# Filling TensorE with wider matmuls between the x transposes and the first projection, with a new scheduler seed

## Chip, cores, metric

One core of a Trainium2 chip. The metric is the device time of one execution in microseconds (us): the median of several runs, all fast unless said otherwise. A profiled run also gives the span from its first to its last instruction, some 1.7 to 2 us shorter than the time.

## The reference

Memory-augmented attention in four segments of 512 tokens, a ReGLU feed-forward network on the same x, and a gate that mixes the two (S = 2048, D = 512, 32 heads, F = 1792, bf16):

```python
x = A_x
g = _sigmoid((x * gate_w).sum(-1, keepdims=True))
a = _A_ref(x, A_wq, A_wk, A_wv, A_wo, A_beta)     # 4 segments: softmax inside one, memory M, z between them
b = _B_ref(x, B_W_gate, B_W_up, B_W_down)         # relu(x @ W_gate) * (x @ W_up) @ W_down
return g * a + (1 - g) * b
# within _A_ref, after each segment s:
M = M + einsum('bhld,bhle->bhde', phi(ks), vs)    # the memory update needs phi(k) transposed
```

## The kernel before

The kernel doesn't fix its order by hand. It describes operations with what they read and write, and a list scheduler, run when the kernel is built, places them on the five engines from estimated durations. Among ready operations of equal priority it adds a random amount drawn from a seed. What comes out is one fixed order for each engine:

```python
sc = Sched(seed=912)
...
def jitter(self, op):
    j = self.jit.get(op.cidx)
    if j is None:
        j = self.jit[op.cidx] = self.rng.random() * 400.0
    return j
```

TensorE starts with fillers (matmuls of constants), transposes the first 512 rows of x against an identity, fills once more, broadcasts gate_w, and begins the q projection:

```python
def warm(m, n, k, b):
    def fn(e):
        for i in range(m):
            ins = e.matmul(PL[:, b, 0:n], lhsT=ones[128, 128], rhs=ones[128, n], start=True, stop=True)   # cut: const_aps
        return ins
    ...
xps, xcs = [warm(5, 512, 0, 3)], []
...                                            # 16 transposes in six groups, each waiting for its part of x
xps.append(warm(3, 128, 1, 2))
xps.append(pe(lambda e: e.matmul(PL[:, 2, :], lhsT=ones[0:1, :], rhs=V.oTt[0:1, :], start=True, stop=True), 300, ..., name="gwx"))
```

SyncE issues nearly all loads, in the order of its program and on one queue (q1 carried 17.69 of the 18.12 MB of the profile), and among them the transposes of phi(k), which are done by DMA, and the transposed x of later segments:

```python
load_gu(0); load_gu(1); load_x(1)
load("sp", ["wo"], V.wo[:], ...)
load("sp", ["wd"], V.wd[:], ...)               # W_down, 1.8 MB, needed only from the first output on
...
sps.append(dma("sp", lambda e, g=g: e.dma_start_transpose(V.phik[:, :, g*128:(g+1)*128], V.ek[:, g, :]), ...))
```

and the memory update (`mu`) is the first reader of the transposed phi(k) on TensorE. ScalarE issues three tiny loads ("touches") of W_gate, W_up and W_down, each waiting for the one before.

## Time and profile before

| | kernel before |
|---|---|
| time, median of 3 | 271.73 us (271.53 to 272.24) |
| span of the profiled run | 269.1 us |
| first q projection | 6.09 us |
| array at full speed from | about 9.5 us |
| the four transposes of phi(k) before the first memory update, issue to landing | 4.2 to 10.3 us |
| longest wait of TensorE after 1 us | 0.8 us, at 18.2 us |

The page, the projection's rows and the start of the chain are shown in the prediction. TensorE's waits (who waited, for whom, us in total, times, longest):

```profile
PE psA L876 <- issue: 2.4, 15, 0.2
PE psL L548 <- PEq L1018: 0.8, 1, 0.8
PE psL L744 <- ACT E L752: 0.8, 1, 0.8
```

The second line is the start of the program. The third is the wait of the scores (L744) for an exponential. The first is fifteen waits, 0.2 us at the longest.

### The profile page before, as it was taken

The page shows a single profiled execution, that of the slowest core. Times are in us where ns is not written, and L with a number is a line of the kernel's source. Part 1 is how long each engine was busy: PE and PEld are TensorE (multiplying, and loading weights), DVE is VectorE, ACT ScalarE, POOL GpSimd, SP SyncE. Part 2 cuts the span into 40 slices and gives each one's busy share as a digit, 9 for nine tenths or more (in the row PEclk, how much of TensorE's full clock was granted, in tenths as well). Part 3 has the DMA queues.
Part 4 walks back from the last instruction along what each step waited for, and adds up shares of the span by engine and source line. Part 5 has one row for each costly group of instructions (what it writes and reads, how often), then busy time and mean ns, then how long its engine had stood idle before and what let it go on. Part 6 is the DMA issues. An engine that isn't in the chain of part 4 may idle for free.

```text
span 269.1 us, 6773 instructions
## 1 busy us (share of the span) xinstructions
PE 260.4 (97%) x2821; PEld 117.3 (44%) x2859; DVE 186.9 (69%) x372; ACT 186.5 (69%) x163; POOL 112.0 (42%) x227
## 2 busy tenths in 40 slices
PE   8989999999999999999999999999999999999996
PEld 3434454444444444444444444444444444444444
DVE  5678796988877497889986858776964437577400
ACT  4368898787799787676877696776776657774122
POOL 3014654486337533864276333822282235421000
PEclk9999999999999999999999999999999999999999
DMA  5899994410023223111012130100212000000011
GB/s 179 230 389 200 322 132 73 97 32 19 23 44 63 49 70 88 50 25 21 2 44 58 41 78 28 39 0 2 44 39 60 20 22 22 0 2 2 0 40 39
DMA packets 34208, 18.12 MB, mean 67 GB/s; under 512 B 23937, under 2 KB 33922, under 8 KB 34178
## 3 DMA queue, kind: packets, MB, share of 16 engines
q1 hardware_dynamic: 34048, 17.69, 27.9%
q8 instruction: 22, 0.36, 0.6%
q14 instruction: 8, 0.07, 0.1%
q10 hardware_dynamic: 130, 0.01, 0.0%
HBM read 9.75 MB, written 2.11 MB: 44 GB/s over the span
## 4 chain that ended last, share of the span: by engine, by line
PE 87%; DMA 4%; SPq 3%; issue 2%; DVE 1%; ACT 1%; ACTq 0%
PE psA L876 36%; PE psA L915 18%; PE psL L744 8%; PE psA L646 7%; PE psA L803 6%; PE psA L908 5%; PE psA L644 3%; DMA adT<-in_B_W_up_dram 2%; SPq L501 1%; PE psA L709 1%; PE psA L811 1%; DMA wq<-in_A_wq_dram 1%; DMA gexpT<-gscr 1%; SPq L670 1%; PE psA L691 1%
## 5 line engine op out<-in xcount | busy, mean ns | idle before, releaser
L752 ACT ACTIVATE E<-psL 128x2048 bf16<-128x2048 f32 x72 | 135.0, 1876 | 30.7 <-PE psL L744 30.3
L770 POOL TENSOR_SCALAR_AFFINE_SELECT E<-E 128x256 bf16<-128x256 bf16 x128 | 52.6, 436 | 105.4 <-ACT E L752 94.3
L876 PE MATMUL psA<-xT,wg 128*128 128x512 bf16 x216 | 57.7, 380 | 1.2 <-issue 1.1
L876 PE MATMUL psA<-xT,wu 128*128 128x512 bf16 x213 | 57.3, 379 | 1.4 <-issue 1.3
L915 PE MATMUL psA<-wd,hT 128*128 128x512 bf16 (+2 forms) x228 | 52.0, 366 | 0.9 <-issue 0.6
L788 POOL TENSOR_SCALAR_AFFINE_SELECT E<-E 64x512 bf16<-64x512 bf16 (+1 forms) x64 | 42.1, 686 | 18.8 <-ACT E L752 10.6
L887 DVE TENSOR_TENSOR hT<-psA,rl 128x512 bf16<-128x512 f32 x56 | 38.2, 682 | 12.1 <-PE psA L876 10.2
L915 PEld LDWEIGHTS psA<-wd,hT 128*128 128x128 bf16 x238 | 21.5, 98 | 23.3 <-issue 1.7
L822 DVE STREAM_TRANSPOSE Tn<-psA 128x512 f32<-128x512 f32 x32 | 21.0, 695 | 14.5 <-PE psA L811 14.3
L876 PEld LDWEIGHTS psA<-xT,wu 128*128 128x128 bf16 x224 | 20.4, 98 | 24.1 <-issue 1.7
L876 PEld LDWEIGHTS psA<-xT,wg 128*128 128x128 bf16 x224 | 19.9, 98 | 24.7 <-issue 2.7
L744 PE MATMUL psL<-qT,kp 32*128 32x64 bf16 (+3 forms) x768 | 28.7, 245 | 0.8 <-ACT E L752 0.8
L884 ACT ACTIVATE rl<-psA 128x512 bf16<-128x512 f32 x28 | 16.7, 596 | 15.6 <-PE psA L876 14.9
L744 PEld LDWEIGHTS psL<-qT,kp 32*128 32x128 bf16 x768 | 9.9, 92 | 31.0 <-issue 18.7
L925 ACT ACTIVATE osb<-psA,omg 128x512 bf16<-128x512 f32 (+2 forms) x13 | 8.5, 655 | 19.9 <-PE psA L908 13.2
L885 DVE TENSOR_SCALAR rl<-psA 128x512 bf16<-128x512 f32 x28 | 19.2, 686 | 4.0 <-PE psA L876 3.2
L646 PE MATMUL psA<-xT,wq 128*128 128x512 bf16 x63 | 17.8, 412 | 0.1
L663 DVE TENSOR_SCALAR kp<-kT,pm 128x512 bf16<-128x512 bf16 (+1 forms) x33 | 11.2, 357 | 9.0 <-PE psL L744 6.8
L803 PE MATMUL psA<-E,vaug 128*17 128x192 bf16 (+3 forms) x512 | 17.0, 273 | 0.1
L646 PE MATMUL psA<-xT,wk 128*128 128x512 bf16 x62 | 16.0, 380 | 0.2 <-issue 0.2
L908 PE MATMUL psA<-wo,oT 128*128 128x512 bf16 (+2 forms) x65 | 15.8, 366 | 0.4 <-issue 0.3
L644 PE MATMUL psA<-wv,xT 128*128 128x512 bf16 x61 | 14.7, 380 | 0.4 <-issue 0.3
(77 smaller groups left out, 235.3 us busy)
## 6 DMA issues: line engine op xcount, KB each, us to landing
out_dram<-osb SPq DMA_DIRECT2D x15, 128.0 KB, 1.8
wg<-in_B_W_gate_dram SPq DMA_DIRECT2D x8, 224.0 KB, 5.7
wu<-in_B_W_up_dram SPq DMA_DIRECT2D x8, 224.0 KB, 5.9
wd<-in_B_W_down_dram SPq DMA_DIRECT2D x1, 1792.0 KB, 10.5
osb<-in_A_x_dram SPq DMA_DIRECT2D x12, 128.0 KB, 2.2
vsh<-vaug SPq DMA_DIRECT2D x4, 272.0 KB, 3.0
hT<-in_A_x_dram SPq DMA_DIRECT2D x4, 128.0 KB, 2.2
wq<-in_A_wq_dram SPq DMA_DIRECT2D x4, 128.0 KB, 3.2
```

The costliest lines, as they stand in the source:

```text
L644: ins = e.matmul(A(ep)[:, :], lhsT=V.xT[:, kt, tok + col * 128:tok + (col + 1) * 128], rhs=w[:, kt, :], start=(kt == 0), stop=(kt == KT - 1))
L646: ins = e.matmul(A(ep)[:, :], lhsT=w[:, kt, col * 128:(col + 1) * 128], rhs=V.xT[:, kt, tok:tok + 512], start=(kt == 0), stop=(kt == KT - 1))
L744: ins = q.matmul(PL[:, jj, o:o + w], lhsT=kap(jj), rhs=V.qT[32 * jj:32 * jj + 32, qs, q0:q0 + w], start=True, stop=True, tile_position=(32 ...
L752: acts.append(act(lambda a, eout=eout: a.activation(eout, PL[:, :, :] if slot is None else PL[:, :, :].rearrange("q h (g c) -> q h g c", g ...
L770: pools.append(pool(lambda g, ap=ap: g.affine_select(out=ap, in_=ap, compare_op=ALU.is_ge, fill=0.0, base=64, pattern=[[0, 4], [1, 64]], c ...
L788: pools.append(pool(lambda e, ap=ap, base=base: e.affine_select(out=ap, in_=ap, compare_op=ALU.is_ge, fill=0.0, base=base, pattern=[[0, 8] ...
L803: ins = q.matmul(A(eps[p])[32 * jj:32 * jj + 17, 512 - w:512], lhsT=V.vaug[:, s % 2, j, 8 * G + 2 * jj + p, :], rhs=V.E[:, e, jj, o:o + w] ...
L822: ds.append(dve(lambda e, p=p, ep=eps[p]: e.transpose(V.Tn[:, p, :], A(ep)[:, :]), t_dve(512), writes=[f"Tn{p}"], name=f"tr{s}_{G}_{p}", e ...
L876: ins = e.matmul(A(ep)[:, :], lhsT=w[:, kt, f * 128:(f + 1) * 128], rhs=V.xT[:, kt, c * 512:(c + 1) * 512], start=(kt == 0), stop=(kt == K ...
L887: evs.append(dve(lambda e, ep=eu, r=r, hs=hs: e.tensor_tensor(V.hT[:, hs, :], A(ep)[:, :], V.rl[:, r, :], ALU.mult), t_dve(512), reads=[f" ...
L908: ins = e.matmul(A(ep)[:, 0:c1 - c0], lhsT=V.oT[:, o0 + G, i * 128:(i + 1) * 128], rhs=V.wo[:, G, c0:c1], start=st_ and G == 0, stop=sp_ a ...
L915: ins = e.matmul(A(ep)[:, 0:c1 - c0], lhsT=V.hT[:, slots[f], i * 128:(i + 1) * 128], rhs=V.wd[:, f, c0:c1], start=st_ and f == f0, stop=sp ...
```

## The change

The intent: up to about 9.5 us TensorE takes 0.427 us for 512 columns, later 0.215 (half speed and full speed), and the change bets that steadier work brings the switch forward. So fill TensorE without a break from the last transpose to the first projection. The 3 x 128 columns ahead of the broadcast go; 512 + 128 + 128 columns come behind it, into a bank of psA that is spare at that time, and with them comes a new seed.

```diff
-    sc = Sched(seed=912)
+    sc = Sched(seed=949)
...
-    xps.append(warm(3, 128, 1, 2))
     xps.append(pe(lambda e: e.matmul(PL[:, 2, :], ...), 300, reads=["oTt"], writes=["bankL2"], name="gwx"))
+
+    def warm1(e):
+        for n in (512, 128, 128):
+            ins = e.matmul(PA[:, 3, 0:n], lhsT=nc.const_aps.tensor(1.0, [128, 128], BF16), rhs=nc.const_aps.tensor(1.0, [128, n], BF16), start=True, stop=True)
+        return ins
+    xps.append(pe(warm1, 400, reads=["init3"], writes=[], name="warm1"))
```

## The prediction

In it "warm" is full speed as measured, 0.215 us for 512 columns. The 0.107 us for 128 columns is the pace at half speed: two transposes of x start at 3.142 and 3.249 us of the same trace. Point 4 and the sum weigh three cases for the switch: ahead of the first projection, 1.1 us earlier than it was (from 4.97 us, where the broadcast would start, to 6.09), and unmoved.

> **What bounds the kernel now.** I read the page first: busy shares, then the slices.
>
> ```profile
> PE 260.4 (97%) x2821; PEld 117.3 (44%) x2859; DVE 186.9 (69%) x372; ACT 186.5 (69%) x163; POOL 112.0 (42%) x227
> PE   8989999999999999999999999999999999999996
> PEclk9999999999999999999999999999999999999999
> ```
>
> TensorE works in nearly every slice; it is idle for 269.1 - 260.4 = 8.7 us of the span. The table of 10 us stretches puts 0.9 of that before 10 us, 0.8 between 10 and 20, 2.4 after 260 (the last outputs draining), so 4.6 us over the 240 us between. The program order is fixed, TensorE is the bound, and a gain must either make matmuls shorter or close idle time. The granted clock says full speed everywhere; whether the matmuls run at full speed has to be read from their own durations. So next the line of the first projections, in the stretches 6 to 9.3 us and 9.6 to 14 us (min/median/max ns):
>
> ```profile
> L646 PE MATMUL psA<-xT,wq x8: 606/631/631, 6.1 to 9.1; 128*128 128x512 bf16 x8
> L646 PE MATMUL psA<-xT,wk x11: 379/379/379, 11.3 to 13.6; 128*128 128x512 bf16 x11
> ```
>
> The same shape takes 631 ns first and 379 ns later. These durations overlap; the pace is read from the weight loads, one per matmul, in the timeline (start, us, what, idle before):
>
> ```profile
> 8.20 0.15 PEld L646 LDWEIGHTS psA<-xT,wq 128*128 128x128 bf16 x1 [0.28 <-issue]
> 8.63 0.15 PEld L646 LDWEIGHTS psA<-xT,wq 128*128 128x128 bf16 x1 [0.28 <-issue]
> 9.05 0.15 PEld L646 LDWEIGHTS psA<-xT,wq 128*128 128x128 bf16 x1 [0.28 <-issue]
> 9.48 1.45 PEld L646 LDWEIGHTS psA<-xT,wq 128*128 128x128 bf16 x7 [0.28 <-issue]
> ```
>
> One per 0.427 us up to 9.48, then seven in 1.45 us, about 0.215 each. The array switches from half to full speed near 9.5 us. Counted back: eight matmuls from 6.12 to 9.53 are slow, the remaining eight of the q projection and everything later is fast. What TensorE did before that, in its timeline:
>
> ```profile
> 0.84 2.29 PE L548 MATMUL psL<-const-bfloat16-1.0 128*128 128x512 bf16 x5 [0.84 <-PEq L1018]
> 2.96 2.21 PE L556 MATMUL psL<-ident,hT 128*128 128x128 bf16 x16
> 4.97 0.52 PE L548 MATMUL psL<-const-bfloat16-1.0 128*128 128x128 bf16 x3
> 5.42 0.60 PE L567 MATMUL psL<-oTt,const-bfloat16-1.0 1*128 1x512 bf16 x1
> 6.09 1.46 PE L646 MATMUL psA<-xT,wq 128*128 128x512 bf16 x3
> ```
>
> Filler, 16 x transposes, filler, the broadcast of gate_w, the first projection. TensorE "busy" hides gaps here[...]. At 0.427 us for 512 columns the broadcast that starts at 5.42 has streamed by 5.85, so the array stands empty 0.24 us until 6.09. Last, the chain of waits up to 18 us:
>
> ```profile
> 2.66 3.38 DMA wq<-in_A_wq_dram
> 6.09 4.05 PE psA L646 x10
> 10.17 5.21 DMA adT<-in_B_W_up_dram
> 15.41 0.36 ACTq L479
> 15.81 0.60 ACT kT L651
> 16.41 1.78 ACT E L752
> 18.23 0.40 PE psL L744 x8
> ```
>
> The first projection starts when the first piece of wq lands (6.04), not when the filler ends. Ten of its matmuls lead to the first q copy on ScalarE; just beside it ScalarE issues a 1 KB load (10.17), whose landing 5.21 us later holds up ScalarE's queue, then a k copy, the first exponential and the second group of scores at 18.23. So the half-speed stretch is on the path that sets the early part, with a nearly fixed delay behind it.
>
> [...] the new filler waits for the memset of bank 3 of psA; the four memsets begin at 0.99 and take 2.11 us, so they are over by 3.1 and the wait costs nothing at 5.4. No later accumulation is hurt, as each starts anew.
>
> **The change part by part.**
> 1. Removed: three fillers of 128 columns between the last transpose and the broadcast. 3 x 0.107 = 0.32 us of streaming; with the change of weights the broadcast started 0.45 us after them.
> 2. Moved: the broadcast comes up to about 4.97, 0.45 us earlier. Its copy on ScalarE (6.06) and the gate products on VectorE (6.69) can come 0.4 to 0.5 us earlier. Neither is on the chain above, so this is worth 0.
> 3. Added: 512 + 128 + 128 columns after the broadcast, 0.427 + 2 x 0.107 = 0.64 us at half speed. Together 0.427 + 0.64 = 1.07 us from 4.97: it ends at 6.04 to 6.1, against the first wq at 6.04. So the first projection moves by 0 to 0.1 us, and if the array is warm already it does not move at all.
> 4. What it is for: [...] eight matmuls at 0.215 instead of 0.427, 8 x 0.212 = 1.7 us gained. [...] the switch comes 1.1 us earlier, and half of that, 0.55 us, is gained. If neither, 0.
> 5. Does the gain get through? wq pieces are issued 0.47 us apart and land 3.0 to 3.4 us after issue, about 6.0 to 7.5; a warm q needs one per 3 x 0.215 = 0.65 us, so it keeps up. wk, issued from 4.56, lands by about 9.3, and a warm q ends at 6.12 + 16 x 0.215 = 9.55, so k keeps up too. The q copy, the 1 KB load behind it and ScalarE's release then move up with it, unless the load is queued behind others and lands at the same time. I take two thirds to all.
> 6. The seed of the scheduler: 912 becomes 949. It changes the random tie-breaks among ready instructions of equal priority on all engines, over all 250 us after. The work on TensorE is the same; what moves is the 4.6 us of scattered idle time plus the early 0.8 us and the tail. I put it at a mean of about +0.2 us gained (a seed is presumably picked because it did well) and a spread of 1 us either way, an estimate from the size of that idle time.
>
> Sum: for the switch, chances of 0.35 for 1.7 us, 0.4 for 0.55 and 0.25 for 0, i.e. 0.8 us; let through for the most part, 0.7; less 0.05 for a late start; plus 0.2 for the seed: about 0.9 us. Of 271.73 that leaves 270.8; I round down to 270.7, since the load behind the q copy may land in less than its 5.21 us when asked for earlier.
>
> **The rivals.**
> - The start is bound by the transfers: wq at 6.04 sets the first projection whatever the filler does, and the 1 KB load's landing sets ScalarE. For it: the chain shows both. Against: between them stand ten matmuls, 4.05 us, eight of them at half speed. If the load lands at 15.4 anyway, the change gives 0 to 0.3 us: 271.4 to 271.8.
> - The filler is too long and holds up the first projection, with the switch at the old time. For it: only 0 to 0.1 us of slack. It would cost at most 0.1 us: 271.8.
> - The seed outweighs the clock: another order makes TensorE wait for an exponential or a bank a few times more or less. For it: these waits are already small and many, the longest on TensorE 0.8 us. It could give 270 to 273 without any effect of the filler.
> - [...] the runs before, 271.53 to 272.24, and the profiled one, 270.94, spread over 1.3 us[...]. Then a median of three carries some 0.4 us of luck.
>
> **Range and chances.** A full early switch with a good seed is 271.7 - 1.7 - 1.2 = 268.8; no effect and a poor seed is 272.2. The range is 268.9 to 272.2. Two per cent is 5.4 us; the slow stretch in all is worth 1.7 us and all of the early idle time not 2, so neither side is likely: faster 0.02, same 0.96, slower 0.02.
>
> **What would show it.** In the changed profile: the broadcast near 4.97 and fillers until about 6.05, no gap before 6.09; weight loads of the first projection at 0.43 us for fewer than eight matmuls[...]; the first q copy at 8.5 to 9.6 instead of 10.17; the 1 KB load's landing and the second group of scores earlier by as much. If the copy comes early but the scores at 18.2 do not move, the transfer hides the gain. If everything up to 20 us is alike and the time differs, it is the seed, and TensorE's idle time after 20 us (8.7 - 1.7 = 7.0 us now) shows by how much. I am wrong if the time leaves the range, above all upward through a new wait in the middle.

## The result, and the profile after

| | before | changed |
|---|---|---|
| time, median of 6 runs each | 271.92 us (271.53 to 272.7) | 269.74 us (269.05 to 270.7) |
| ratio | | 0.9917, 95% interval 0.9892 to 0.9942 |
| span of the profiled run | 269.1 us | 267.3 us |

Ratios here and below are the mean time of one kernel's fast runs over the mean of the other's in the same rounds, so they are not quite the ratio of the medians. The change gains 2.2 us, 0.8%: inside the predicted range, and over twice the predicted 1.0 us.

At first sight the profile shows just what was intended. The page's first line and slices of the changed kernel:

```profile
PE 262.7 (98%) x2859; PEld 117.2 (44%) x2859; DVE 189.1 (71%) x371; ACT 187.6 (70%) x164; POOL 112.3 (42%) x227
PE   8999998999999999999999999999999999999996
PEclk9999999999999999999999999999999999999999
```

and its weight loads on TensorE (start, us, what, idle before):

```profile
5.02 0.09 PEld L566 LDWEIGHTS psL<-oTt,const-bfloat16-1.0 1*128 1x128 bf16 x1
5.33 0.33 PEld L570 LDWEIGHTS psA<-const-bfloat16-1.0 128*128 128x128 bf16 x3 [0.23 <-issue]
5.63 3.18 PEld L651 LDWEIGHTS psA<-xT,wq 128*128 128x128 bf16 x16
```

All sixteen q matmuls stand about 0.215 us apart, none 0.427: the array is fast from the first projection on. But look at the first two lines. The broadcast of 512 columns starts at 5.02, and 0.31 us later the fillers (L570) start: at half speed 512 columns alone take 0.427 us. (The record of the broadcast itself is 0.38 us long, against 0.60 in the kernel before.) The array was already fast when the first of the new fillers began. In this run the switch was not their work.

The chain up to 18 us has no wait for a transfer any more, only TensorE itself:

```profile
5.41 0.44 PE psA L570 x3
5.84 6.04 PE psA L651 x28
11.89 0.33 PE psL L749 x8
```

The last thing to see is what the early start buys. The first k projection's weights are loaded at 8.92 instead of 11.05 us, 2.1 us earlier, and the wait for the exponential at 18.2 us is gone. Together that is 2.9 us, yet the span shrinks by 1.8. The list of TensorE's waits says where the rest went:

```profile
PE psL L548 <- PEq L1023: 0.8, 1, 0.8
PE psA L651 <- DMA xT<-in_A_x_dram: 0.8, 1, 0.8
PE psA L808 <- DVE vaug L678: 0.5, 1, 0.5
```

At 43.5 us it waits 0.8 us for the transposed x of the third segment, and at 47.0 us 0.5 us for a copy on VectorE: new waits, 1.3 us. Part of the gain is given back.

This list is complete, and the fifteen waits for "issue" have no counterpart in it. The reason stands in the page's first line: 2859 matmul records for 2859 weight loads here, 2821 for 2859 in the kernel before. Those 0.2 us "waits" are holes left by the 38 missing records, not idle time.

### The profile page after: what moved, and what is told of

Its sections match the earlier page's. It is cut to its first block, busy times and chain, and to the rows that moved or that the text cites.

```text
span 267.3 us, 6812 instructions
## 1 busy us (share of the span) xinstructions
PE 262.7 (98%) x2859; PEld 117.2 (44%) x2859; DVE 189.1 (71%) x371; ACT 187.6 (70%) x164; POOL 112.3 (42%) x227
## 4 chain that ended last, share of the span: by engine, by line
PE 94%; SPq 2%; DVE 2%; DMA 1%; issue 0%; ACT 0%
PE psA L881 37%; PE psA L920 19%; PE psA L651 9%; PE psL L749 8%; PE psA L808 6%; PE psA L913 5%; PE psA L649 4%; PE psA L816 1%; DMA xT<-in_A_x_dram 1%; PE psA L714 1%; SPq L501 1%; SPq L675 1%; PE psL L548 1%; PE psA L696 1%; PE psL L556 0%
## 5 line engine op out<-in xcount | busy, mean ns | idle before, releaser
L881 PE MATMUL psA<-xT,wg 128*128 128x512 bf16 x224 | 59.6, 380 | 0.0
L881 PE MATMUL psA<-xT,wu 128*128 128x512 bf16 x224 | 59.3, 380 | 0.0
L920 PE MATMUL psA<-wd,hT 128*128 128x512 bf16 (+2 forms) x238 | 54.0, 367 | 0.0
L892 DVE TENSOR_TENSOR hT<-psA,rl 128x512 bf16<-128x512 f32 x56 | 38.1, 680 | 13.3 <-PE psA L881 12.6
L889 ACT ACTIVATE rl<-psA 128x512 bf16<-128x512 f32 x32 | 19.1, 597 | 17.0 <-PE psA L881 16.9
L930 ACT ACTIVATE osb<-psA,omg 128x512 bf16<-128x512 f32 (+2 forms) x12 | 7.8, 652 | 18.0 <-PE psA L913 13.2
L890 DVE TENSOR_SCALAR rl<-psA 128x512 bf16<-128x512 f32 x24 | 16.5, 688 | 3.5 <-PE psA L881 2.4
L651 PE MATMUL psA<-xT,wq 128*128 128x512 bf16 x64 | 16.2, 380 | 0.8 <-DMA xT<-in_A_x_dram 0.8
L913 PE MATMUL psA<-wo,oT 128*128 128x512 bf16 (+2 forms) x68 | 16.5, 367 | 0.0
L649 PE MATMUL psA<-wv,xT 128*128 128x512 bf16 x64 | 15.5, 380 | 0.0
L668 DVE TENSOR_SCALAR kp<-kT,pm 128x512 bf16<-128x512 bf16 (+1 forms) x33 | 12.3, 387 | 4.1 <-PE psL L749 3.8
```

The lines of the kernel that those rows point to most:

```text
L649: ins = e.matmul(A(ep)[:, :], lhsT=V.xT[:, kt, tok + col * 128:tok + (col + 1) * 128], rhs=w[:, kt, :], start=(kt == 0), stop=(kt == KT - 1))
L651: ins = e.matmul(A(ep)[:, :], lhsT=w[:, kt, col * 128:(col + 1) * 128], rhs=V.xT[:, kt, tok:tok + 512], start=(kt == 0), stop=(kt == KT - 1))
L881: ins = e.matmul(A(ep)[:, :], lhsT=w[:, kt, f * 128:(f + 1) * 128], rhs=V.xT[:, kt, c * 512:(c + 1) * 512], start=(kt == 0), stop=(kt == K ...
L892: evs.append(dve(lambda e, ep=eu, r=r, hs=hs: e.tensor_tensor(V.hT[:, hs, :], A(ep)[:, :], V.rl[:, r, :], ALU.mult), t_dve(512), reads=[f" ...
L913: ins = e.matmul(A(ep)[:, 0:c1 - c0], lhsT=V.oT[:, o0 + G, i * 128:(i + 1) * 128], rhs=V.wo[:, G, c0:c1], start=st_ and G == 0, stop=sp_ a ...
L920: ins = e.matmul(A(ep)[:, 0:c1 - c0], lhsT=V.hT[:, slots[f], i * 128:(i + 1) * 128], rhs=V.wd[:, f, c0:c1], start=st_ and f == f0, stop=sp ...
```

## The experiments

Twelve kernels ran in three calls of four. Those of one call share a chip and the runs of the kernel before. "Switch" is the time at which the spacing of the weight loads of q goes from 0.43 to 0.215 us, read from the one profiled run of each kernel; where all sixteen are at 0.215 ("early"), it came before the first.

| run | order of | fillers | median us | ratio to before | span | switch |
|---|---|---|---|---|---|---|
| before | before | old | 271.73 | 1 | 269.1 | 9.5 |
| changed kernel | change | new | 269.74 | 0.9917 | 267.3 | by 5.3 |
| newsched_oldfill | change | old | 269.54 | 0.9932 | 267.8 | 9.9 |
| oldsched_newfill | before | new | 271.09 | 0.9988 | 269.2 | 10.0 |
| newsched_nofill | change | none | 269.06 | 0.9918 | 268.1 | 9.8 |
| after_again | change | new | 269.53 | 0.9929 | 268.8 | 9.8 |
| newsched_dense | change | denser | 269.38 | 0.9901 | 267.6 | early |
| newsched_nofill_xT_touch | change | none | 270.01 | 0.9926 | slow | early |
| newsched_dense_xT_touch | change | denser | 271.46 | 0.9963 | 270.6 | early |
| oldsched_touch | before | old | 272.2 | 0.9998 | 271.3 | early |
| oldsched_wd | before | old | 268.04 | 0.9868 | 266.0 | early |
| newsched_nofill_wd | change | none | 267.5 | 0.9860 | 266.4 | early |
| before_again | before | old | 272.48 | 1.0018 | 270.7 | early |
| before_seed949 | a third one | old | 276.41 | 1.0169 | 274.8 | early |

The runs of the kernel before had medians of 271.55, 272.27 and 271.14 us in the three calls.

### First call: order against fillers

The change does two things, and the seed reorders every engine. To part them, the order must be held fixed while the fillers change. That is possible because the scheduler sees only the estimated duration of an operation, not what it emits. So the fillers were put inside operations that exist anyway; the resulting instruction lists are the same on all engines but for the fillers. (`ones` stands for the constant operands in the diffs, which are shortened.) This gives all four cells of order and fillers.

**newsched_oldfill**, the changed kernel's order with the old fillers:

```diff
-    xps.append(pe(lambda e: e.matmul(PL[:, 2, :], ...), 300, ..., name="gwx"))
+    xps.append(pe(lambda e: [*[e.matmul(PL[:, 2, 0:n], ones, ones) for n in (128, 128, 128)], e.matmul(PL[:, 2, :], ...)][-1], 300, ..., name="gwx"))
-        for n in (512, 128, 128):
+        for n in (8,):
```

> The changed kernel's instruction order on every engine (seed 949), but the fillers as in the kernel before: three of 128 columns ahead of the gate_w broadcast, and only one of 8 columns behind it. If the fillers work (they warm the array's clock earlier in most runs), this gives back most of the 2.2 us: 271.0 to 272.0, and in the profile half-speed projections (0.43 us apart) until 8.5 to 10 us. If the new order does the work, it stays at the changed kernel's 269.7, within 0.4 us. [...]

Measured: 269.54 us (269.01 to 270.25), ratio 0.9932 with an interval of 0.99 to 0.9964. The change's gain without the change's fillers.

**oldsched_newfill**, the old order with the new fillers:

```diff
-            for i in range(m):
-                ins = e.matmul(PL[:, b, 0:n], ...)
+            for i in range(m if k == 0 else 1):
+                ins = e.matmul(PL[:, b, 0:n if k == 0 else 8], ...)
-    xps.append(pe(lambda e: e.matmul(PL[:, 2, :], ...), 300, ..., name="gwx"))
+    xps.append(pe(lambda e: [e.matmul(PL[:, 2, :], ...), *[e.matmul(PA[:, 3, 0:n], ones, ones) for n in (512, 128, 128)]][-1], 300, ..., name="gwx"))
```

> The order of the kernel before on every engine (seed 912), but the fillers of the change: 8 columns ahead of the broadcast, 512 + 128 + 128 behind it. If the fillers work: 270.0 to 270.8, and fewer than eight slow projections in the profile. If the order does the work: 271.9 as before, within 0.4 us.

Measured: 271.09 us (270.47 to 272.48), ratio 0.9988, interval 0.9949 to 1.0027: the time of before.

**newsched_nofill**, nothing but 8 columns after the broadcast:

```diff
-        for n in (512, 128, 128):
+        for n in (8,):
```

> The changed kernel without any filler between the last transpose and the first projection but one of 8 columns; all orders as in the changed kernel. If filling that stretch matters for the clock, this is the slowest of the new order: 1 us or more above the changed kernel (270.7 to 271.7)[...]. If it does not, 269.4 to 270.0.

Measured: 269.06 us (268.85 to 269.96), ratio 0.9918. Without any filler it is no slower than with them.

**after_again**, the changed kernel unaltered:

> The changed kernel unaltered, for a second profile and for times on the same chip in the same rounds. Median 269.7 within 0.4. [...] the switch to full speed will not stand at 5.0 us again as in the first profile, but anywhere between 4.5 and 8.5.

Measured: 269.53 us (268.03 to 270.68), ratio 0.9929. The expectation of the switch failed: it came at 9.8 us, later than the 4.5 to 8.5 it named. The same kernel that was fast from its first projection had its first eight q matmuls at half speed here. Its weight loads:

```profile
9.16 0.15 PEld L651 LDWEIGHTS psA<-xT,wq 128*128 128x128 bf16 x1 [0.28 <-issue]
9.58 0.15 PEld L651 LDWEIGHTS psA<-xT,wq 128*128 128x128 bf16 x1 [0.28 <-issue]
9.90 1.39 PEld L651 LDWEIGHTS psA<-xT,wq 128*128 128x128 bf16 x7 [0.17 <-issue]
```

Those of newsched_oldfill, for comparison:

```profile
9.47 0.15 PEld L651 LDWEIGHTS psA<-xT,wq 128*128 128x128 bf16 x1 [0.28 <-issue]
9.89 1.18 PEld L651 LDWEIGHTS psA<-xT,wq 128*128 128x128 bf16 x6 [0.27 <-issue]
```

All four kernels of this call, with four kinds of filling, switch between 9.8 and 10.0 us. So two things follow. The order carries the gain, at either filling. And in these profiles the fillers don't set the switch: it stands nearly still, whatever fills the stretch.

What the order does in these late-switch runs shows only in part. The spans of the old order are 269.1 and 269.2, of the new one 267.8, 268.1 and 268.8: 0.9 us in the mean. TensorE waits for an exponential near 18 to 20 us in the old order 0.8 and 0.9 us, in the new one not at all, 0.4 and 0.7 us. In the old order two more spots, at 123 and 173 us, have two weight loads 0.51 us apart instead of 0.22, 0.3 us each; they are absent in the new order. But 0.9 is not 2.2; the clocks of the runs without a profile, at the end of the experiments, close part of the gap.

### Second call: force an early switch, and look behind it

Theory at this point: the early switch happens in some runs, and its gain is partly swallowed at 43 us. **newsched_dense** fills the gaps between the transposes, so that TensorE stops less there (from 3.04 to 5.24 us its weight loads show no stop, those of newsched_nofill three, of 0.27, 0.22 and 0.20 us); the change's own fillers shrink to 8 columns, as in newsched_nofill:

```diff
+FILLS = {"xt2": (192, "L"), "xt3": (160, "L"), "gwx": (128, "A"), "warm1": (128, "A")}
     for g in gs:                      # groups of waits and one operation, in program order
+        if e == "pe" and _name(g) in FILLS:
+            _fill(eng, sc, *FILLS[_name(g)])     # a matmul of ones, ahead of the operation's waits
         yield from g
```

> The changed kernel's orders, with fillers in the gaps between the x transposes (192 and 160 columns ahead of the third and fourth, 128 on either side of the broadcast) in place of the change's 512 + 128 + 128. [...] this should bring the switch to full speed forward from 9.6 to 9.9 us (five of six profiles so far) to 5 to 6.6 in the profile. If that early switch goes through to the end, 1 us or more below the kernel without fillers (269.06): 267.6 to 268.4. If it is swallowed by the transposed loads of x that the third segment waits for at 43 us, 268.6 to 269.4 with a wait there. [...]

Measured: 269.38 us (269.22 to 269.9), ratio 0.9901, the switch early. Its waits on TensorE:

```profile
PE psA L651 <- DMA xT<-in_A_x_dram: 0.6, 1, 0.6
PE psA L808 <- DVE vaug L678: 0.5, 1, 0.5
PE psA L696 <- DMA phik<-ek: 0.2, 1, 0.2
```

The expectation "swallowed" holds: 0.9901 is not clearly below the 0.9918 of the kernel without fillers (its interval reaches from 0.9886 to 0.995), and x is waited for. But the early switch can't be credited to the fillers, since the other three kernels of this call, one of them with the old fillers untouched, were early too. Whether denser filling moves a late switch is not tested: no dense kernel ran where the others were late.

Two more kernels of this call add edits off TensorE. ScalarE's wait for the landing of the W_up touch comes seven instructions later ("touch"), and the third segment's transposed loads are issued ahead of the second pair of phi(k) transposes ("xT"):

```diff
+    if e == "act":
+        n = [i for i, g in enumerate(gs) if _name(g) == "ldadT"][-1]
+        held, gs[n] = gs[n][:-1], gs[n][-1:]
+        gs[n + 7] = held + gs[n + 7]
+    if e == "sp":
+        x = [g for g in gs if _name(g).startswith("ldx2_")]
+        gs = [g for g in gs if g not in x[1:]]
+        n = gs.index(x[0])
+        gs[n + 1:n + 1] = x[1:]
```

**newsched_nofill_xT_touch**:

> No fillers, the changed kernel's orders, but for two edits off TensorE: ScalarE waits for the landing of the W_up touch seven instructions later, and the queue of SyncE issues the last three transposed loads of the third segment's x ahead of two transposes of phi(k). If ScalarE's wait for the touch is what stops TensorE near 18 to 20 us (0.3 to 0.9 us), 268.5 or so, against 269.06 without the edits, and no stall above 0.3 us there. If that wait is beside the path: 269.0 within 0.4.

Measured: 270.01 us over all runs, ratio of the fast ones 0.9926. A miss in us, and by its ratio the two edits together changed nothing against newsched_nofill's 0.9918.

**newsched_dense_xT_touch**:

> Both: the denser fillers and the two edits. If the early switch of the clock is real and was swallowed at 43 us, this is the fastest of all, 267.0 to 267.8, with no wait for x at 43 us. If the switch does not come early, as the kernel without fillers and with the edits, or 0.2 us slower.

Measured: 271.46 us, ratio 0.9963: meant to be the fastest and 2 us slower than newsched_dense. The expectation was wrong, and the trace shows something useful. Its weight loads:

```profile
39.65 0.11 PEld L649 LDWEIGHTS psA<-wv,xT 128*128 128x128 bf16 x2 [0.21 <-DVE mutmp L699]
42.76 0.48 PEld L696 LDWEIGHTS psA<-vaug,phik 128*128 128x128 bf16 x8 [3.00 <-issue]
43.20 0.37 PEld L649 LDWEIGHTS psA<-wv,xT 128*128 128x128 bf16 x3
43.75 0.15 PEld L649 LDWEIGHTS psA<-wv,xT 128*128 128x128 bf16 x1 [0.17 <-issue]
44.18 0.15 PEld L649 LDWEIGHTS psA<-wv,xT 128*128 128x128 bf16 x1 [0.28 <-issue]
```

Putting x first made the second pair of phi(k) late (the chain has one issued at 38.95 us and landed at 41.40; the changed kernel issues the pair from 33.81 us); TensorE stood still before the memory update (L696), 2.5 us by the list of its waits, and afterwards the loads are 0.43 us apart: the array has fallen back to half speed. Here a long wait cost twice, once as idle time and once as slow matmuls.

**oldsched_touch**, the old order with the ScalarE edit alone:

> The kernel before with one edit: ScalarE waits for the landing of the W_up touch seven instructions later; the order of every engine is the same. If the stall of TensorE at 18.2 us (0.9 us in both profiles of this order) comes from that wait and is part of what the new order removes: 0.6 to 1.0 us below before, 270.6 to 271.0, and no stall at 18 us. If ScalarE is late there for another reason: as before within 0.3.

Measured: 272.2 us (270.72 to 273.22), ratio 0.9998. With the early switch the wait near 18 us did not occur, so there was nothing to remove. But the trace has a wait of 3.3 us for phi(k) at 38.7 us, which the profile of before does not have. Is it the edit, or the old order at an early switch? The third call asks.

### Third call: the appointment

New theory: phi(k) lands at a time that the transfers set, not TensorE. In the old order TensorE comes for it just in time when the switch is late. When the switch is early it comes 2 to 3 us too soon, waits, and drops to half speed, so that the early switch is worse than none. From the first projection on, the new order has ten more matmuls of 512 columns (124 against 114) ahead of the first memory update, 10 x 0.216 = 2.2 us more to do until then.

**before_again**, the kernel before unaltered:

> The kernel before, unaltered, for a second profile. [...] its switch stands where the other three of this call have it. If that is early (about 5 us), theory: a wait of 2 to 3.5 us for phi(k) near 36 to 38 us with matmuls at half speed after it, span 269.5 to 271.5 in spite of the early switch. If the wait was made by the ScalarE edit of the earlier run, no such wait, span below 268.

Measured: 272.48 us (271.52 to 272.71), ratio 1.0018, profiled run 272.71 us with a span of 270.7, early switch. Its weight loads:

```profile
34.52 0.12 PEld L744 LDWEIGHTS psL<-qT,kp 32*128 32x128 bf16 x8 [0.42 <-ACT kp L665]
38.20 0.82 PEld L691 LDWEIGHTS psA<-vaug,phik 128*128 128x128 bf16 x8 [3.56 <-DMA phik<-ek]
38.98 0.27 PEld L646 LDWEIGHTS psA<-xT,wq 128*128 128x128 bf16 x2
39.52 0.15 PEld L646 LDWEIGHTS psA<-xT,wk 128*128 128x128 bf16 x1 [0.28 <-issue]
39.95 0.15 PEld L646 LDWEIGHTS psA<-xT,wk 128*128 128x128 bf16 x1 [0.28 <-issue]
```

and the stretches around it (PE, PEld, DVE, ACT, POOL busy, then the granted clock, DMA share and GB/s):

```profile
34.00:38.00 4.00, 0.92 (x11) 0.21 (x9) 1.49 (x3) 0.21 (x1) 1.12 (x3) 1.00 1.37 172
38.00:42.00 4.00, 3.77 (x21) 2.21 (x22) 1.34 (x3) 3.43 (x3) 1.54 (x3) 0.57 0.61 131
```

What the theory expects to see is there: the wait for phi(k) (3.3 us in the list of waits), the half-speed loads after it, and a granted clock of 0.57 from 38 to 42 us. The first k weights were loaded at 8.78 us, 2.3 us ahead of the first profile of this kernel, and it ended 1.6 us behind it. The ScalarE edit is cleared.

One part of the theory does not hold: the landing is not fixed. The memory update needs the first two transposes of phi(k). In the first profile of this kernel (late switch) they were issued at 25.5 and 29.7 us and landed at 35.8 and 36.3, which left 1.6 us until TensorE came, at 37.9. Here (early switch) they were issued at 25.4 and 31.1 and landed at 37.7 and 38.1, while TensorE stood ready at 34.9. So of the wait some 1.4 us come from TensorE's earlier arrival and 1.8 us from the later landing. In the changed kernel the second landed at 37.1 us, 0.1 us before TensorE needed it, against 35.7 in newsched_nofill with its late switch. Why they land later is open; the late and the early profiles of a kernel also come from different calls.

In the changed kernel with its early switch the same point reads

```profile
37.20 0.48 PEld L696 LDWEIGHTS psA<-vaug,phik 128*128 128x128 bf16 x8
```

with no wait ahead of it. So the old order spans 270.7 us at an early switch and the new one 267.3 and 267.6: 3.3 us between them in the mean, against 0.9 at a late switch. The 2.2 us of the medians lie between.

**oldsched_wd** asks what makes phi(k) late. In the old order SyncE issues the 1.8 MB of W_down just ahead of it; the edit moves that load behind the reads of gexpT, and nothing else:

```diff
+    if e == "sp":
+        wd = [g for g in gs if _name(g) == "ldwd"][0]
+        gs.remove(wd)
+        n = [i for i, g in enumerate(gs) if _name(g) == "grd0"][0]
+        gs.insert(n + 1, wd)
```

> The kernel before with one edit in SyncE's queue: the 1.8 MB load of W_down is issued behind the gexpT reads (about 42 us) instead of ahead of the first transposes of phi(k) (25 us). TensorE, VectorE, ScalarE and GpSimd keep their orders. Theory (the clock's gain meets a fixed appointment: in the old order TensorE needs transposed phi(k) at 35 us when the array is at full speed early, and it lands at 38): phi(k) lands 2 us or more earlier, so with an early switch the 3.3 us wait and the second slow stretch go, and the time falls to 268.0 to 269.5; with a late switch there is little to wait for, 270.5 to 271.3. Rival (phi(k) is late because of its own producers, VectorE and ScalarE, or SyncE's issue time): no change, 271.5 to 272.3.

Measured: 268.04 us (267.75 to 268.31), ratio 0.9868, interval 0.9836 to 0.99. The four transposes of phi(k) before the first memory update took, from issue to landing, in the first profile of before, and in before_again:

```profile
DMA to landing us min/median/max: 4.2/6.6/10.3
DMA to landing us min/median/max: 4.2/7.0/12.2
```

and in oldsched_wd:

```profile
DMA to landing us min/median/max: 5.5/6.6/6.8
```

TensorE no longer waits for them, and stays fast (oldsched_wd, weight loads):

```profile
34.79 0.12 PEld L744 LDWEIGHTS psL<-qT,kp 32*128 32x128 bf16 x8 [0.42 <-ACT kp L665]
35.12 0.47 PEld L691 LDWEIGHTS psA<-vaug,phik 128*128 128x128 bf16 x8 [0.21 <-issue]
```

The 12.2 us were the first transpose: issued at 25.44 us, landed at 37.65, when W_down, issued at 24.77, was done as well (12.4 us to its landing). That the small transfer (128 KB by its shape) waits behind the large one here is our reading; the edit, which moves nothing but the large one, bears it out: 6.8 us at most, against 10.3 and 12.2. The old seed, the old fillers and one load moved gain at least as much as the change: 0.9868 against its 0.9917, measured in different calls, with intervals that just overlap.

**newsched_nofill_wd**, the new order without fillers and with the same move:

> The changed kernel's orders without fillers, and the W_down load moved in the same way. Theory: the waits for x at 43 us (0.7 to 0.9 us with an early switch) and what hangs on slow landings there shrink: 267.2 to 268.4, the fastest of all. Rival: SyncE's own issue times (1.26 us for each transposed load) set these landings: 268.9 to 269.5 as without the move.

Measured: 267.5 us (267.27 to 269.44), ratio 0.986, interval 0.9822 to 0.9899: the lowest median of all, 3.6 us below the 271.14 of before in this call. Between the two orders there is now no clear difference, 0.9868 against 0.986. The waits for phi(k) and for x at 43 us are gone; one of 0.8 us for VectorE at 54.9 us is new.

**before_seed949**, the old source with only the seed of the change:

```diff
-    sc = Sched(seed=912)
+    sc = Sched(seed=949)
```

> The kernel before with the seed of the change and the old fillers, so a third order of its own, neither that of before nor that of the change. If the seed itself carried the gain: 269.5 like the changed kernel. If each order is a draw of its own: anything from 269 to 273, and the verdict on the change is that of one lucky draw.

Measured: 276.41 us (275.11 to 277.08), ratio 1.0169, interval 1.0123 to 1.0215. Its waits on TensorE:

```profile
PE psA L691 <- DMA phik<-ek: 3.0, 1, 3.0
PE psA L709 <- DVE amem L718: 1.2, 1, 1.2
PE psL L744 <- ACT E L752: 1.0, 2, 0.8
```

The same seed that goes with the change's gain makes the old source 1.7% slower. So the gain does not belong to the seed as such; it belongs to the order that this source and this seed give together, which the scheduler draws anew for each pair. This draw meets phi(k) too early as well, and collects more waits near 80 us. Its matmuls stay fast after the 3.0 us wait; the half-speed stretch comes later, at 81 to 84 us (loads 0.43 us apart, a granted clock of 0.50 from 82 to 84), after waits of 0.8 and 1.2 us close together. A wait's length alone does not decide: the loads were 0.43 us apart after 2.5 us in newsched_dense_xT_touch and after 3.3 us in before_again, while after the 3.0 us here the eight loads of the next half of the memory update took 0.67 us, as in the changed kernel.

### The clocks of the runs without a profile

Each run's mean granted clock says more than one profile for each kernel can. The four profiles of the fast state with a clock of 0.994 have a half-speed stretch somewhere after the start; the nine with 1.000 have none. (An estimate: 0.994 over 270.7 us is some 3.2 us at half speed.) The half-speed start is not in this clock: it reads 1.00 in all of the first 10 us of the kernel before, and 0.57 at 38 to 42 us of before_again. So the spacing of the weight loads is the safer reading. The fast runs of the kernel before split in each call:

| call | clock 0.993 or 0.994: runs, mean us | clock 0.999 or 1.000: runs, mean us |
|---|---|---|
| first | 4, 272.3 | 6, 270.9 |
| second | 5, 272.7 | 6, 271.7 |
| third | 5, 272.5 | 6, 270.8 |

None of the 36 runs of the new order with SyncE's queue unchanged or with W_down moved is below 1.000, nor any of the six of oldsched_wd. So the gain of the order has two parts. In the first call its three kernels average 269.5 us: 2.9 us less than the runs of before that lost the clock, and 1.4 us less than those that did not. The first part is, if the profiles of before_again and oldsched_touch stand for these runs, the long wait and what follows it; the second is only in part explained (the 0.9 us above).

It also warns of reading the switch from one profile. In the profiles of the old order with SyncE's queue unchanged 0.994 comes with an early switch and 1.000 with a late one. If that holds for the other runs, the first call had early switches too, in 4 of 10 runs of before and in 1 of 6 of oldsched_newfill, though all its four profiles are late. No trace of these runs is kept, so this is not shown.

## Why the prediction was right or wrong

The time was in the range and "within 2%" was right, with 1.0 us forecast and 2.2 measured. The reasons were for the most part wrong, so the hit was luck: the gain that was forecast from the clock came from the order. The rival that fits best, "The seed outweighs the clock", was on the list, but was given +0.2 us in the sum.

1. "The array switches from half to full speed near 9.5 us", and the half-speed stretch is worth 1.7 us: right as a reading. In the early profile of the changed kernel k starts 2.1 us earlier, of which the clock is 1.7.
2. "What it is for: ... eight matmuls at 0.215 instead of 0.427, 8 x 0.212 = 1.7 us gained": this step, an estimate from the start, failed. With the order held, new fillers on the old order gave 0.9988, and old ones or none on the new order gave 0.9932 and 0.9918. In the profiles the switch stood at 9.8 to 10.0 us with all four fillings of the first call and ahead of the first projection with all eight kernels of the other two (one of these profiles is slow). It does not follow the filling. Of the rivals the last, with runs of one kernel that "spread over 1.3 us", is the nearest to this; whether an early or late switch goes with the call, as the profiles look, or changes from run to run, as the clocks suggest, is open.
3. "Does the gain get through? ... I take two thirds to all": failed, and this is the most useful error. It was checked only up to the k projection. Behind that stand landings that don't come earlier when TensorE does: x at 43 us, and phi(k), which even came later (38.1 us against 36.3 in the old order). In the new order about 1.3 us are given back, of the 2.1 gained at k and 0.8 at the exponential; in the old order all of it and 1.6 us more, because the long wait was followed by half-speed matmuls.
4. "The first projection moves by 0 to 0.1 us": this rests on wq landing at 6.04, which only that profile shows. Its first piece took 3.38 us to land there; the pieces took 2.1 to 2.8 in newsched_nofill, oldsched_newfill and after_again. With the late switch q started at 5.76 us without fillers, at 6.07 with the old ones, and at 6.20 and 6.49 with the new ones. At half speed they delay what they should help.
5. The seed, "a mean of about +0.2 us gained ... and a spread of 1 us either way": mis-sized. The order alone measured about 2 us (0.9932 with the old fillers, 0.9918 with none), and the same seed on the old source is 1.7% slower (1.0169). The estimate came from "4.6 us of scattered idle time", and much of that was not idle at all but missing matmul records; and it left out that a new order also shifts TensorE against late transfers and can keep or lose the clock.
6. "The 1 KB load's landing sets ScalarE", for the wait near 18 us: seen in the late-switch chain, and absent with an early switch. The test of it met an early switch and settled nothing.

Open stays what sets the time of the switch, why the profiles of one call agreed, why phi(k) landed later with an early switch, and how many of the runs without a profile were early. So the 2.2 us can't be split exactly into late and early runs, and of the 1.4 us between the undisturbed runs of the two orders at least 0.5 have no cause found.

## What to carry to other kernels

When a change comes with a new seed or a new order, hold the order fixed and vary the content alone, and the reverse, before crediting either; a profile in which the intended effect is present doesn't show that the change made it. Ask of each microsecond gained early which fixed landing it will meet next: time gained ahead of a late transfer was lost there (1.3 us in the changed kernel), and a long wait can cost the clock too (waits of 2.5 and 3.3 us did, one of 3.0 us did not). Issue a large load that is needed late behind the small ones that are needed soon (0.9868 here).
